# Decode attention over a KV cache: the V transfers are issued from GpSimd's software queue instead of the SP queue

## The chip, the cores and the metric

One core of one Trainium2 chip. The metric is the device time of one execution in microseconds (us).

## The reference

Four layers, alternating between two sets of weights and caches (A, B, A, B). Each has one query token, 32 heads, a head size of 192 and a cache of 8192 positions:

```python
q = layernorm(x) @ wq                  # 640 -> 32 heads x 192
scores = q . k_cache * 192 ** -0.5     # per head, 8192 positions
p = softmax(scores)
o = p @ v_cache
x = x + o @ wo                         # 6144 -> 640
```

Everything is in bfloat16. Nothing of a cache is used twice in a layer, so per head 3.146 MB of K and 3.146 MB of V come from HBM and are used once. Over four layers K and V make 805 MB, the weights 63 MB.

## The kernel before

Every engine has an explicit program of operations and semaphore waits. K and V each have three buffers ("slots") of one head. SP issues all transfers. Cuts are marked with `...`.

```python
def sp_k(h, Kt=Kt):
    i = counters["k"] % NKSLOT                 # NKSLOT = 3
    counters["k"] += 1
    SP.wait(T["kslot"][i])                     # until VectorE is done with head h-3
    ...
    return i, SP.op(f, sem=semK[i], inc=16)    # one transfer of 128 rows of 24,576 bytes

def sp_v(h, Vt=Vt):
    i = counters["v"] % NVSLOT                 # NVSLOT = 3
    counters["v"] += 1
    SP.wait(T["vslot"][i])                     # until TensorE has used V of head h-3
    ...
    return i, SP.op(f, sem=semV[i], inc=16)

# start of a layer (layers 1 to 3)
ev_wq[0], ev_wq[1] = ...                       # two pieces of wq
need_k(0); need_k(1); need_v(0); need_k(2)
ev_wo[0] = sp_wo(0)
# layer normalisation: VectorE, with one power operation on GpSimd
e = PO.op(lambda g: g.tensor_tensor(stat[0:1, 4:5], stat[0:1, 3:4], neghalf[0:1, 0:1], ALU.pow))
...
for h in range(HRUN):
    need_k(h); need_k(h + 1); ...; need_v(h)   # issues what is not issued yet
    cur = stage_tree_a(h, ki, ev_k)            # VectorE: K slot *= q   (waits for K of head h)
    if h >= 1: stage_M(heads[h - 1])
    if h >= 2: stage_out_dve(heads[h - 2])
    stage_tree_a2(cur)                         # VectorE: first halving of the sum
    if h >= 1: stage_softmax(heads[h - 1], ...)  # exponent; TensorE: 64 products with V of head h-1
    stage_act_rows(cur)
    if h >= 2: stage_out(heads[h - 2])         # TensorE: output projection
    stage_tree_b(cur)                          # VectorE: rest of the sum, maximum; frees the K slot
```

So V of head h is needed after VectorE's multiplication for head h+1, about 23 us later than K of head h.

Of the kernel before, what the change touches and what calls it, by code (L numbers as in the profile page):

```python
# [115 lines left out]
def build(nc, A_x, A_k, A_v, A_wq, A_wo, B_x, B_k, B_v, B_wq, B_wo, out, dbg=None, cfg=None):  # L116
# [34 lines left out]
    with ExitStack() as ctx:  # L151
        def sb(name, shape, dt):
            return ctx.enter_context(nc.sbuf_tensor(name, shape, dt))
# [4 lines left out]
        def sem(name):  # L158
            return ctx.enter_context(nc.semaphore(name))

        kslot = [sb(f"kslot{i}", [128, JJ * DH], BF16) for i in range(NKSLOT)]
        vslot = [sb(f"vslot{i}", [128, JJ * DH], BF16) for i in range(NVSLOT)]
# [46 lines left out]
        semV = [sem(f"semV{i}") for i in range(NVSLOT)]  # L209
# [6 lines left out]
        SP = Stream("SP", None)  # L216
# [3 lines left out]
        PO = Stream("POOL", pPOOL)  # L220
# [32 lines left out]
        for i_ in range(2):  # L253
# [5 lines left out]
        T = dict(  # L259
            kslot=[None] * NKSLOT,  # L260
            vslot=[None] * NVSLOT,
            wq=[None] * 2,
            wo=[None] * 2,
            qb=[None, None],
            qslot=[None] * 8,
            sa=[None, None],
            ob=[None, None],
# [16 lines left out]
        for l in range(NL):  # L284
# [30 lines left out]
            def sp_v(h, Vt=Vt):  # L315
                i = counters["v"] % NVSLOT
                counters["v"] += 1
                SP.wait(T["vslot"][i])
                def f(s, i=i, h=h):
                    return s.dma_start(vslot[i][:, :], Vt[0, h].rearrange("(p j) d -> p (j d)", p=128))  # L320
                return i, SP.op(f, sem=semV[i], inc=16)

            ev_wq = [None] * NPAIR
            ev_wo = [None] * NG
# [8 lines left out]
            def need_v(h):  # L333
                if h >= H:
                    return
                if ("v", h) not in kv:
                    kv[("v", h)] = sp_v(h)
# [428 lines left out]
```

## Time and profile before

| what | value | view |
|---|---|---|
| time | 2074.65 us | median of 2 runs |
| DMA engines | busy 9 tenths or more in 39 of 40 slices | slices |
| VectorE / TensorE busy | 85% / 56% | busy table |
| VectorE waiting for K | 213 us in all | waits |
| TensorE waiting for V | 4.4 us in all | waits |
| issue to landing, K / V | 32.6 / 36.1 us | issues |

From the page of the kernel before: the span, busy time by engine (busy us, share, instructions), the DMA share in tenths and GB/s for 40 equal slices, the SP queue (packets, MB, share of 16 engines' span), and the chain of waits by engine.

```profile
span 2073.2 us, 24389 instructions
PE 1158.3 (56%) x9625; PEld 915.1 (44%) x9668; DVE 1764.8 (85%) x1190; ACT 596.1 (29%) x3254; POOL 3.1 (0%) x13
...
DMA  9999999999999999999999999999999999999995
GB/s 395 430 425 428 422 422 427 426 430 419 423 426 425 427 422 424 426 426 428 418 423 426 423 429 424 422 427 426 426 410 425 425 423 424 423 423 425 426 427 254
...
q1 hardware_dynamic: 77700, 868.24, 99.3%
...
DMA 45%; issue 25%; DVE 24%; PE 4%; ACT 1%; SPq 1%; POOL 0%; POOLq 0%; DVEq 0%; ACTq 0%
```

The DMA engines are the bound: they hardly rest, at about 424 GB/s. VectorE, the next busiest, works about 13.8 us per head and waits for K in the rest.

The waits of the kernel before (who waited for whom: us in total, times, longest):

```profile
DVE kslot L463 <- DMA kslot<-in_A_k_cache_dram: 116.6, 56, 8.2
DVE kslot L463 <- DMA kslot<-in_B_k_cache_dram: 96.6, 49, 6.8
...
PE OB L557 <- DMA vslot<-in_B_v_cache_dram: 4.4, 5, 0.9
```

VectorE waits for most heads' K, TensorE waits a little for V.

The chain of waits of the kernel before, its last part (start us, us, what):

```profile
2010.75 32.68 DMA kslot<-in_B_k_cache_dram
2043.45 6.56 DVE kslot L463
```

VectorE starts on the last K (head 31 of layer 3) at 2043.45 us, and the kernel ends 29.7 us later. Between lie that multiplication, the softmax and V product of head 30, then those of head 31.

### The profile page before, as it was taken

The page shows a single profiled execution, that of the slowest core. Times are in us where ns is not written, and L with a number is a line of the kernel's source. Part 1 is how long each engine was busy: PE and PEld are TensorE (multiplying, and loading weights), DVE is VectorE, ACT ScalarE, POOL GpSimd, SP SyncE. Part 2 cuts the span into 40 slices and gives each one's busy share as a digit, 9 for nine tenths or more (in the row PEclk, how much of TensorE's full clock was granted, in tenths as well). Part 3 has the DMA queues.
Part 4 walks back from the last instruction along what each step waited for, and adds up shares of the span by engine and source line. Part 5 has one row for each costly group of instructions (what it writes and reads, how often), then busy time and mean ns, then how long its engine had stood idle before and what let it go on. Part 6 is the DMA issues. An engine that isn't in the chain of part 4 may idle for free.

```text
span 2073.2 us, 24389 instructions
## 1 busy us (share of the span) xinstructions
PE 1158.3 (56%) x9625; PEld 915.1 (44%) x9668; DVE 1764.8 (85%) x1190; ACT 596.1 (29%) x3254; POOL 3.1 (0%) x13
## 2 busy tenths in 40 slices
PE   2565556555465555566536565556563665556656
PEld 1444444444354444444425454445452454444444
DVE  7888888988698888898779888889878988888896
ACT  2222232232232322232223332223222332223232
POOL 0000000000000000000000000000000000000000
PEclk7777777877678777777767777777776777777877
DMA  9999999999999999999999999999999999999995
GB/s 395 430 425 428 422 422 427 426 430 419 423 426 425 427 422 424 426 426 428 418 423 426 423 429 424 422 427 426 426 410 425 425 423 424 423 423 425 426 427 254
DMA packets 77813, 869.79 MB, mean 420 GB/s; under 512 B 4994, under 2 KB 29572, under 8 KB 44932
## 3 DMA queue, kind: packets, MB, share of 16 engines
q1 hardware_dynamic: 77700, 868.24, 99.3%
q8 instruction: 76, 1.25, 0.2%
q14 instruction: 37, 0.30, 0.0%
HBM read 868.22 MB, written 0.00 MB: 419 GB/s over the span
## 4 chain that ended last, share of the span: by engine, by line
DMA 45%; issue 25%; DVE 24%; PE 4%; ACT 1%; SPq 1%; POOL 0%; POOLq 0%; DVEq 0%; ACTq 0%
DMA kslot<-in_B_k_cache_dram 28%; DMA kslot<-in_A_k_cache_dram 17%; DVE kslot L463 12%; DVE kslot L504 5%; DVE kslot L492 4%; PE OB L557 3%; DVE s_sb L508 1%; SPq L312 0%; DVE M_sb L530 0%; DVE m_sb L515 0%; PE QB L412 0%; PE YL L632 0%; ACT p_sb L547 0%; DVE rl_sb L572 0%; SPq L295 0%
## 5 line engine op out<-in xcount | busy, mean ns | idle before, releaser
L463 DVE TENSOR_TENSOR kslot<-kslot,q_sb 128x12288 bf16<-128x12288 bf16 x128 | 839.3, 6557 | 226.2 <-DMA kslot<-in_A_k_cache_dram 116.6
L557 PE MATMUL OB<-vslot,p_sb 128*1 128x192 bf16 x8192 | 951.1, 294 | 84.3 <-ACT p_sb L547 78.6
L557 PEld LDWEIGHTS OB<-vslot,p_sb 128*1 128x1 bf16 x8192 | 809.6, 101 | 205.7 <-ACT p_sb L547 93.5
L539 PE MATMUL SA<-M_bf,ones_bf 1*128 1x1 bf16 x128 | 22.9, 179 | 689.2 <-ACT M_bf L537 689.2
L504 DVE TENSOR_TENSOR kslot<-kslot 128x2688 bf16<-128x2688 bf16 (+2 forms) x384 | 374.4, 975 | 13.3
L492 DVE TENSOR_TENSOR kslot<-kslot 128x5376 bf16<-128x5376 bf16 x128 | 374.7, 2927 | 0.1
L481 ACT ACTIVATE kslot<-kslot 128x192 bf16<-128x192 bf16 x1024 | 355.3, 348 | 22.2 <-DVE kslot L463 22.2
L539 PEld LDWEIGHTS SA<-M_bf,ones_bf 1*128 1x128 bf16 x128 | 12.4, 97 | 725.0 <-ACT M_bf L537 725.0
L537 ACT ACTIVATE M_bf<-M_sb 1x1 bf16<-1x1 f32 x128 | 26.5, 207 | 666.3 <-DVE M_sb L530 666.3
L481 ACT ACTIVATION_READ_ACCUMULATOR kslot<-kslot 128x1 f32 x1024 | 192.1, 188 | 0.0
L508 DVE TENSOR_REDUCE s_sb<-kslot 128x56 f32<-128x672 bf16 x128 | 109.1, 852 | 4.4
L632 PE MATMUL YL<-wo,oT_sb 128*1 128x512 bf16 x256 | 83.0, 378 | 51.8 <-ACT oT_sb L609 31.7
L605 ACT ACTIVATE oT_sb<-OB 128x1 bf16<-128x1 f32 x64 | 11.2, 175 | 310.9 <-PE OB L593 310.9
L608 ACT ACTIVATE oT_sb<-OB 64x1 bf16<-64x1 f32 x64 | 10.9, 170 | 281.0 <-PE OB L597 281.0
L412 PE MATMUL QB<-wq,xT_b 128*128 128x512 bf16 x197 | 57.5, 426 | 11.2 <-issue 6.4
L523 PE MATMUL SA<-ident,m_bf 128*1 128x128 bf16 x128 | 28.2, 221 | 54.5 <-ACT m_bf L520 54.5
L632 PEld LDWEIGHTS YL<-wo,oT_sb 128*1 128x1 bf16 x256 | 20.7, 81 | 79.7 <-ACT oT_sb L609 37.2
L634 PE MATMUL YH<-wo,oT_sb 128*1 128x128 bf16 x256 | 55.9, 218 | 0.0
L425 ACT ACTIVATE q_sb<-QB 128x512 bf16<-128x512 f32 x48 | 28.7, 598 | 93.6 <-PE QB L412 93.6
L578 ACT ACTIVATE orow_bf<-OB,rl_sb 1x192 bf16<-1x192 f32 x128 | 51.0, 399 | 1.7 <-DVE rl_sb L572 1.7
L547 ACT ACTIVATE p_sb<-s_sb,negm_sb 128x64 bf16<-128x64 f32 x128 | 44.8, 350 | 4.1
L530 DVE TENSOR_REDUCE M_sb<-SA 1x1 f32<-1x128 f32 x128 | 34.7, 271 | 12.6 <-PE SA L523 12.6
(50 smaller groups left out, 368.9 us busy)
## 6 DMA issues: line engine op xcount, KB each, us to landing
kslot<-in_A_k_cache_dram SPq DMA_DIRECT2D x64, 3072.0 KB, 32.6
vslot<-in_A_v_cache_dram SPq DMA_DIRECT2D x64, 3072.0 KB, 36.1
kslot<-in_B_k_cache_dram SPq DMA_DIRECT2D x64, 3072.0 KB, 32.6
vslot<-in_B_v_cache_dram SPq DMA_DIRECT2D x64, 3072.0 KB, 36.3
wq<-in_A_wq_dram SPq DMA_DIRECT2D x12, 1280.0 KB, 24.9
wo<-in_A_wo_dram SPq DMA_DIRECT2D x16, 960.0 KB, 38.2
wq<-in_B_wq_dram SPq DMA_DIRECT2D x12, 1280.0 KB, 25.7
wo<-in_B_wo_dram SPq DMA_DIRECT2D x16, 960.0 KB, 38.6
```

The costliest lines, as they stand in the source:

```text
L412: return t.matmul(QB[nb % 2][:, 0:ncols], lhsT=xT_b[:, c, :], rhs=wq_buf[s_][:, c, (nb % 2) * 512:(nb % 2) * 512 + ncols], start=(c == 0), ...
L463: e = DV.op(lambda v, k3=k3, qb_ap=qb_ap: v.tensor_tensor(k3, k3, qb_ap, ALU.mult))
L481: ea = AC.op(lambda a, k3=k3, par=par, j=j: a.activation(k3[:, j, :], k3[:, j, :], ACT.Copy, accum_out=s_sb[par][:, j:j + 1]))
L492: e = DV.op(lambda v, kt=kt, hw_=hw_: v.tensor_tensor(kt[:, :, 0:hw_], kt[:, :, 0:hw_], kt[:, :, hw_:DH], ALU.add))
L504: e = DV.op(lambda v, kt=kt, hw_=hw_, w=w: v.tensor_tensor(kt[:, :, 0:hw_], kt[:, :, 0:hw_], kt[:, :, hw_:w], ALU.add))
L508: cur["s"] = DV.op(lambda v, kt=kt, par=par, w=w, JA=JA: v.tensor_reduce(s_sb[par][:, JA:JJ], kt[:, :, 0:w], AX.X, ALU.add))
L539: cur["negM"] = PE.op(lambda t, par=par: t.matmul(SA[par][:, SA_NEGM:SA_NEGM + 1], lhsT=ones_bf[0:1, 0:128], rhs=M_bf[par][0:1, 0:1], star ...
L547: cur["p"] = AC.op(lambda a, par=par: a.activation(p_sb[par][:], s_sb[par][:], ACT.Exp, bias=negm_sb[par][:], scale=C))
L557: return t.matmul(OB[par][0:1, 0:DH], lhsT=p_sb[par][:, j:j + 1], rhs=vs3[:, j, :], start=(j == 0), stop=(j == JJ - 1))
L578: cur["orow"] = AC.op(lambda a, par=par: a.activation(orow_bf[par][:], OB[par][0:1, 0:DH], ACT.Copy, scale=rl_sb[par][0:1, 0:1]), tag=(f"O ...
L632: return t.matmul(YL[0:1, 0:512], lhsT=lhsT, rhs=rhs[:, 0:512], start=st, stop=sp_)
L634: return t.matmul(YH[0:1, 0:D - 512], lhsT=lhsT, rhs=rhs[:, 512:D], start=st, stop=sp_)
```

## The change

The intent: SP issues everything in one program order, so a V transfer whose slot is not free holds up the K transfer behind it, and the other way round. GpSimd is idle (busy 3.1 us). Giving it the V transfers lets each stream wait for its own slots only.

```diff
             def sp_v(h, Vt=Vt):
                 i = counters["v"] % NVSLOT
                 counters["v"] += 1
-                SP.wait(T["vslot"][i])
+                PO.wait(T["vslot"][i])
                 def f(s, i=i, h=h):
                     return s.dma_start(vslot[i][:, :], Vt[0, h].rearrange("(p j) d -> p (j d)", p=128))
-                return i, SP.op(f, sem=semV[i], inc=16)
+                return i, PO.op(f, sem=semV[i], inc=16)
```

## The prediction

> **What bounds the kernel.** The DMA engines. The slices show DMA at 9 tenths in all but the last, mostly 422 to 430 GB/s; the queue table gives the SP queue 99.3% of 16 engines' span. VectorE is busy 85%, TensorE 56%. The chain of waits is 45% "DMA into kslot", and the waits view has VectorE waiting 213 us for K and TensorE only 4.4 us for V. Per head VectorE works about 13.8 us; K and V (3.146 MB each) take about 14.8 us together at 424 GB/s, near 16 us with the weights. Packet records: a K or V row is one 24,576-byte packet of 915 ns; the 1,280- and 2,048-byte weight packets take 58 and 87 ns.
>
> **What the change does.** No byte and no compute instruction is removed; VectorE, ScalarE and TensorE keep their order. 128 of SP's 306 commands move to GpSimd; SP's saving is not on the path, as the queue behind it is never empty.
>
> What moves is order. Before, K and V are served first in, first out. After, each engine alternates between two queues packet by packet (the Trainium skill, "DMA: Bandwidth & Descriptors", section "Queues, rings and completion order"; no run shows it yet). K and V packets are equal, so they share half and half; V runs ahead until its three slots are full. Against small weight packets V takes nearly the whole engine, so the first weights, and K behind them, come later (by up to some 15 us), DMA still busy. The GpSimd stream also holds the power operation of each layer's normalisation, so V of heads 1 and 2 of a layer waits for it. At the first boundary the timeline gives about 9 MB outstanding at VectorE's last reduction (517 us); 7.2 MB can move before the power operation (534 us): little or no bubble.
>
> **What of it is on the path.** In the body, DMA stays saturated, so the time per head stays. The end changes: before, the last K is used at 2043.5 us and DMA ends near 2052.5 us, V last; then VectorE, softmax and the V product run to 2073. After, the last K and V share the engines, so K can land up to 8 to 9 us later, and everything after it too: my estimate +7 us. Start and boundaries: +0 to +8. Descriptor work on GpSimd is hidden by three slots. VectorE runs almost only two-input tensor operations and reductions here; the skill's "SBUF — State Buffer", section "Who interferes with whom", infers these do not block descriptor writing.
>
> **Predicted time: 2084 us, 8 in 10 within 2066 to 2114.** Faster by over 2%: 0.02; within 2%: 0.85; slower by over 2%: 0.13.
>
> **What would show it.** A second, software queue with about 403 MB; 24,576-byte packets in both; body slices still 420 to 430 GB/s; VectorE's multiplication still 6.56 us; the last K in use near 2050, not 2043.5; no new waits of TensorE for V.
>
> **What would make it wrong.** (1) Software descriptors cut a row into smaller packets: fitting the packet times gives about 12 ns fixed each, so 4 KB packets would cost V about 6%, some 60 us: slower. (2) Descriptor writing is held off by VectorE's nearly continuous work: TensorE would wait for V and DMA would show holes. (3) GpSimd holds up VectorE: its operations would lengthen beyond the 2 us of slack per head. (4) DMA holes at the layer boundaries. (5) Two queues overlap better and lift the rate above 430 GB/s: faster, at most about 1%.

## More of the kernel before

The DMA issues of the kernel before (KB each, median us from issue to landing):

```profile
kslot<-in_A_k_cache_dram SPq DMA_DIRECT2D x64, 3072.0 KB, 32.6
vslot<-in_A_v_cache_dram SPq DMA_DIRECT2D x64, 3072.0 KB, 36.1
```

Stretches of 5 us in the second layer, 20 to 35 us after its first multiplication (busy us and instructions by engine, TensorE clock, DMA share, GB/s):

```profile
core 0: us, PE busy (x) PEld busy (x) DVE busy (x) ACT busy (x) POOL busy (x), PEclk, DMA share, GB/s
560.00:565.00 5.00, 3.88 (x25) 3.02 (x26) 4.93 (x4) 3.50 (x19) 0.00 (x0) 0.50 1.05 417
565.00:570.00 5.00, 3.89 (x44) 3.59 (x42) 4.90 (x5) 0.52 (x3) 0.00 (x0) 0.94 1.01 426
```

The DMA share stays at 1: there is no hole after the pause between two layers.

## The result, and the profile after

2096.3 us (2 runs: 2095.62 and 2096.99), correct. The ratio to the kernel before is 1.0104, with a 95% interval of 1.0075 to 1.0133. Ratios in this document are the mean time of one kernel's fast runs over that of the other's fast runs of the same rounds, so not quite the ratio of the medians that are quoted.

From the page of the kernel after, the lines that answer to those of before:

```profile
span 2093.8 us, 24432 instructions
PE 1153.6 (55%) x9668; PEld 909.6 (43%) x9668; DVE 1760.3 (84%) x1190; ACT 593.7 (28%) x3254; POOL 71.6 (3%) x141
...
DMA  9999999999999999999999999999999999999993
GB/s 400 423 428 427 424 420 428 428 426 421 421 393 427 425 425 422 427 425 430 421 391 428 425 427 423 424 425 425 427 424 390 426 424 423 430 424 425 427 425 162
...
q1 hardware_dynamic: 59268, 465.58, 53.4%
q0 software_dynamic: 18432, 402.66, 45.0%
```

Same bytes, same busy time, same rate in most slices. Four slices are lower: those with 393, 391 and 390 GB/s, one near the start of each of layers 1 to 3, and the last one (162 against 254).

The waits of the kernel after:

```profile
DVE kslot L463 <- DMA kslot<-in_A_k_cache_dram: 134.3, 27, 19.6
DVE kslot L463 <- DMA kslot<-in_B_k_cache_dram: 102.6, 26, 13.0
```

VectorE's wait for K grew from 213 to 237 us, in half as many and longer waits. TensorE's wait for V is no longer in the list.

The issues of the kernel after:

```profile
kslot<-in_A_k_cache_dram SPq DMA_DIRECT2D x64, 3072.0 KB, 30.1
vslot<-in_A_v_cache_dram POOLq DMA_DIRECT2D x64, 3072.0 KB, 19.6
```

V now lands 19.6 us after its issue instead of 36.1, though nobody waited for it before. K hardly gained.

The chain of waits of the kernel after, its last part:

```profile
2029.88 33.74 DMA kslot<-in_B_k_cache_dram
2063.64 6.56 DVE kslot L463
```

The last K is used at 2063.64 us, 20.2 us later than before; the rest of the kernel takes 30.1 us, against 29.7 before. So nearly all of the loss of 20.6 us lies ahead of that point.

Stretches after the first multiplication of the second layer (now at 553.7 us):

```profile
core 0: us, PE busy (x) PEld busy (x) DVE busy (x) ACT busy (x) POOL busy (x), PEclk, DMA share, GB/s
570.00:575.00 5.00, 0.18 (x1) 0.10 (x1) 5.00 (x3) 0.54 (x3) 0.00 (x0) 0.50 1.02 419
575.00:580.00 5.00, 4.77 (x31) 3.84 (x32) 4.90 (x4) 2.94 (x17) 0.00 (x0) 0.52 0.71 305
580.00:585.00 5.00, 2.97 (x38) 2.81 (x35) 4.93 (x4) 0.51 (x3) 0.53 (x1) 1.00 0.65 211
585.00:590.00 5.00, 1.26 (x9) 0.95 (x9) 5.00 (x4) 1.85 (x10) 0.00 (x0) 0.67 0.98 423
```

Here are the holes: a DMA share of 0.71 and 0.65 while VectorE is fully busy.

**Where the 20.6 us of the two profiles are.** The following is worked out from the trace: a transfer has landed when its semaphore gets its sixteenth increment; "early" is the mean time from landing to use, over heads 3 to 31 of each layer (use of K: VectorE's multiplication starts; use of V: the exponent that feeds the product ends).

| | before | after |
|---|---|---|
| K early | 0.4 us | 2.8 us |
| V early | 0.8 us | 20.3 us |
| last K or V transfer lands (DMA ends) | 2058.0 us | 2064.5 us |
| last K used | 2043.5 us | 2063.6 us |
| last K used before DMA ends | 14.5 us | 0.9 us |
| span after DMA ends | 15.2 us | 29.3 us |

DMA ends 6.5 us later, and what is left after it is 14.1 us longer; together 20.6. The first is for the most part the holes: from the packet records, between 20 us and DMA's end, the idle time of the engines came to 8.2 us before (5.0 of it in the last 10 us) and 13.4 after (2.6 in the last 10 us). So the holes outside the last 10 us grew from 3.2 to 10.8 us, the engines' idle time in the last 10 us shrank, and 1.3 of the 6.5 us are not accounted for by idle time. The second is the order at the end: before, the last V landed last; after, the last K landed 0.9 us before DMA ends.

**How the queues share an engine.** The packet records show it best at the start of the kernel after. The number of packets that ended in each stretch:

| stretch | V queue, 24,576-byte packets | SP queue, packets |
|---|---|---|
| 12 to 16 us | 35 | 36 of K, 24,576 bytes |
| 26 to 28 us | 32 | 32 of wq, 2,048 bytes |
| 30 to 32 us | 32 | 32 of wq, 2,048 bytes |

As many packets of one queue are served as of the other, whatever their sizes. Beside K, V gets half of the bytes. Beside wq, V gets 92% (24,576 of 26,624 bytes), and the K transfers that stand behind wq in the SP queue wait as long. V of head 0 had landed at 21.4 us and was first used at 57.6. The second piece of wq landed at 39.8 us instead of 18.2, and the first multiplication started at 26.2 us instead of 14.8.

### The profile page after: what moved, and what is told of

Read it like the earlier page. It is cut to its first block, busy times and chain, and to the rows that moved or that the text cites. A ratio compares the mean times of both kernels' runs of the same rounds, so it can differ in the third digit from the quotient of the medians.

```text
span 2093.8 us, 24432 instructions
## 1 busy us (share of the span) xinstructions
PE 1153.6 (55%) x9668; PEld 909.6 (43%) x9668; DVE 1760.3 (84%) x1190; ACT 593.7 (28%) x3254; POOL 71.6 (3%) x141
## 4 chain that ended last, share of the span: by engine, by line
DVE 46%; DMA 46%; PE 6%; ACT 1%; issue 1%; SPq 0%; POOL 0%; DVEq 0%; ACTq 0%
DMA kslot<-in_A_k_cache_dram 25%; DVE kslot L463 24%; DMA kslot<-in_B_k_cache_dram 21%; DVE kslot L504 9%; DVE kslot L492 9%; PE OB L557 5%; DVE s_sb L508 3%; DVE M_sb L530 1%; DVE m_sb L515 1%; PE QB L412 1%; PE YL L632 0%; ACT p_sb L547 0%; DVE rl_sb L572 0%; ACT M_bf L537 0%; SPq L295 0%
## 5 line engine op out<-in xcount | busy, mean ns | idle before, releaser
L557 PE MATMUL OB<-vslot,p_sb 128*1 128x192 bf16 x8192 | 938.9, 292 | 82.1 <-ACT p_sb L547 82.1
L537 ACT ACTIVATE M_bf<-M_sb 1x1 bf16<-1x1 f32 x128 | 26.2, 204 | 689.7 <-DVE M_sb L530 689.7
L608 ACT ACTIVATE oT_sb<-OB 64x1 bf16<-64x1 f32 x64 | 10.8, 168 | 273.2 <-PE OB L597 273.2
L412 PE MATMUL QB<-wq,xT_b 128*128 128x512 bf16 x240 | 67.8, 423 | 7.4 <-DMA wq<-in_A_wq_dram 4.7
L320 POOL DMA_DIRECT2D vslot<-in_A_v_cache_dram x64 | 34.3, 537 | 944.0 <-PE OB L593 443.9
L320 POOL DMA_DIRECT2D vslot<-in_B_v_cache_dram x64 | 34.2, 535 | 936.6 <-PE OB L593 457.6
## 6 DMA issues: line engine op xcount, KB each, us to landing
kslot<-in_A_k_cache_dram SPq DMA_DIRECT2D x64, 3072.0 KB, 30.1
vslot<-in_A_v_cache_dram POOLq DMA_DIRECT2D x64, 3072.0 KB, 19.6
```

The lines of the kernel that those rows point to most:

```text
L320: return s.dma_start(vslot[i][:, :], Vt[0, h].rearrange("(p j) d -> p (j d)", p=128))
L412: return t.matmul(QB[nb % 2][:, 0:ncols], lhsT=xT_b[:, c, :], rhs=wq_buf[s_][:, c, (nb % 2) * 512:(nb % 2) * 512 + ncols], start=(c == 0), ...
L557: return t.matmul(OB[par][0:1, 0:DH], lhsT=p_sb[par][:, j:j + 1], rhs=vs3[:, j, :], start=(j == 0), stop=(j == JJ - 1))
```

## The experiments

The theories, as they stood ahead of the first run:

- **A, the order of service.** A second queue lets V run ahead of K. V fills its slots with data that nobody needs yet; K comes last at the end, and after a layer's pause DMA runs out of free slots. Who fills the queue is immaterial.
- **B, the software queue itself**: descriptor work on GpSimd, its port to SBUF, its packets.
- **C, GpSimd's program**: V of heads 1 and 2 of a layer waits behind the power operation, and that makes the holes.
- **D** (came up later), **a second queue as such**: alternation costs, whatever each queue holds.

All runs gave correct results and were timed for 5 rounds. The kernel before ran in the same rounds. "Early", "DMA ends" and "last K" are worked out as above, from the one profiled execution of each run.

| run | median us | ratio to before (95%) | K early | V early | DMA ends | last K used before DMA ends |
|---|---|---|---|---|---|---|
| before | 2075.22 to 2075.66 | | 0.4 | 0.8 | 2058.0 | 14.5 |
| c0_after_again | 2094.92 | 1.0094 (1.0080 to 1.0108) | 2.7 | 20.9 | 2066.9 | 0.1 |
| e1_v_act | 2097.66 | 1.0108 (1.0093 to 1.0124) | 3.5 | 19.5 | 2063.6 | -1.0 |
| e2_all_gpsimd | 2076.75 | 1.0007 (0.9995 to 1.0020) | 0.4 | 0.8 | 2059.5 | 14.5 |
| e3_v_before_pow | 2093.31 | 1.0087 (1.0072 to 1.0103) | 2.8 | 20.5 | 2064.9 | 2.5 |
| e4_gate_ends | 2084.62 | 1.0047 (1.0034 to 1.0059) | 3.1 | 19.4 | 2059.1 | 7.5 |
| e5_gate_last | 2089.61 | 1.0070 (1.0057 to 1.0084) | 2.9 | 20.4 | 2065.7 | 7.6 |
| e6_gate_inner | 2089.95 | 1.0073 (1.0059 to 1.0086) | 2.8 | 19.6 | 2059.1 | 0.9 |
| e9_gate_k_same | 2081.90 | 1.0032 (1.0020 to 1.0045) | 1.9 | 5.3 | 2059.2 | 8.5 |
| e8_gate_k_next | 2078.65 | 1.0014 (1.0001 to 1.0026) | 7.8 | -1.8 | 2058.1 | 10.6 |
| e7_gate_start | 2098.76 | 1.0111 (1.0096 to 1.0126) | 3.0 | 20.4 | 2069.3 | 1.7 |
| e10_k_alone_sp | 2092.33 | 1.0084 (1.0069 to 1.0099) | 12.2 | -0.8 | 2074.0 | 9.3 |
| e11_k_alone_gpsimd | 2094.48 | 1.0091 (1.0075 to 1.0108) | 12.2 | -1.1 | 2072.3 | 9.7 |

### The change again, with more rounds

No edit.

> The changed kernel unaltered, as a control with more rounds: 1.0104 times the kernel before (about 2096 us), as the first two runs gave. All theories agree.

2094.92 us over four runs (2090.75 to 2098.15). The loss is well clear of noise; single runs of this kernel differ by up to 7.4 us, where those of the kernel before stay within 1.3 in the same rounds.

### V from ScalarE's hardware queue

```diff
-                PO.wait(T["vslot"][i])
+                AC.wait(T["vslot"][i])
 ...
-                return i, PO.op(f, sem=semV[i], inc=16)
+                return i, AC.op(f, sem=semV[i], inc=16)
 ...
             T["sa"][0] = ev_xTb
+            need_v(1); need_v(2)
 ...
                     stage_out_dve(heads[h - 2])
+                    need_v(h + 1)        # right after ScalarE has waited for that V product anyway
```

The two added calls keep the moment of issue close to that of the change: within 5.1 us for all V but the first of layers 1 to 3, which came some 26 us later here.

> V from ScalarE's hardware queue, issued at the same moments as GpSimd issues it in the changed kernel (after the V product that frees the slot). Theory A (the order of service: a second queue lets V run ahead of K, whoever fills it): the loss stays, 2090 to 2102 us, DMA holes of about 3 us after each layer start, the last K in use 20 us later than before. Rival B (the software queue itself: descriptor work on GpSimd, its port, its packets): back to 2072 to 2080 us.

2097.66 us. The queue table and an issue line of this run:

```profile
q1 hardware_dynamic: 59268, 465.58, 53.4%
q10 hardware_dynamic: 18432, 402.66, 45.0%
...
vslot<-in_A_v_cache_dram ACTq DMA_DIRECT2D x64, 3072.0 KB, 19.5
```

No software queue is left, and the loss is whole: V again lands 19.5 us after issue, and the last K is used after DMA has ended. Rival B can't explain this run.

### Everything from GpSimd's software queue

```diff
 def sp_wq, sp_wo:
-                QE = AC if cfg.get("...", False) else SP
+                QE = PO
 def sp_k:
-                SP.wait(T["kslot"][i])
+                PO.wait(T["kslot"][i])
 ...
-                return i, SP.op(f, sem=semK[i], inc=16)
+                return i, PO.op(f, sem=semK[i], inc=16)
```

> K, V and both weights all from GpSimd, so one queue again, first in first out, in the order of the kernel before, but all through the software queue. Theory A: back to 2072 to 2082 us. Rival B: twice the bytes through the software queue, so the loss at least stays, 2096 to 2120 us.

2076.75 us; the interval of the ratio includes 1. The queue table and the issues:

```profile
q0 software_dynamic: 51584, 868.24, 99.0%
...
kslot<-in_A_k_cache_dram POOLq DMA_DIRECT2D x64, 3072.0 KB, 32.4
vslot<-in_A_v_cache_dram POOLq DMA_DIRECT2D x64, 3072.0 KB, 38.3
```

All 868 MB through the software queue cost at most 0.2%. With one queue, first in first out, K and V are as early as before (0.4 and 0.8 us), and the last K is used 14.5 us before DMA ends, as before. This run and the one above it turn each other's two properties round: the kind of queue is immaterial, the number of queues is not. B has fallen.

### V ahead of the power operation

```diff
-                need_k(1); need_v(0); need_k(2)
+                need_k(1); need_v(0); need_k(2); need_v(1); need_v(2)      # layer 0; so also in the others
```

> The changed kernel with V of heads 1 and 2 of each layer ahead of the power operation in GpSimd's stream, so that nothing holds them but their slots. Theory A (order of service): nothing gained, 2091 to 2099 us, holes after each layer start as before. Rival C (the power operation holds them and makes the holes): the holes go, 2084 to 2090 us.

2093.31 us. In the second layer V of heads 1 and 2 was now issued at 532.72 and 542.66 us; in the change both followed the power operation at 548.84. The same stretches of this run:

```profile
575.00:580.00 5.00, 4.36 (x29) 3.39 (x29) 4.90 (x4) 3.28 (x18) 0.00 (x0) 0.50 0.68 290
580.00:585.00 5.00, 3.33 (x41) 3.15 (x38) 4.93 (x4) 0.51 (x3) 0.57 (x1) 0.99 0.55 167
```

The hole is no smaller than in the change. A likely reason, not tested, is that what is issued earlier also lands earlier, and so leaves nothing more to do when DMA runs dry. C has fallen.

### A gate at the end of each layer, and its two parts

The gate holds V of heads 29 to 31 until K that is needed sooner has landed. It only adds waits.

```diff
                 PO.wait(T["vslot"][i])
+                if h >= H - 3:                                   # e4_gate_ends
+                if h >= H - 3 and l == NL - 1:                   # e5_gate_last, instead
+                if h >= H - 3 and l < NL - 1:                    # e6_gate_inner, instead
+                    PO.wait(kv[("k", min(h + 1, H - 1))][1])
```

All layers:

> The changed kernel, still V on the software queue, but in each layer V of head 29 also waits until K of head 30 has landed, and V of heads 30 and 31 until K of head 31 has. Theory A: K of head 31 lands sooner in each layer, the DMA holes after the layer starts and the longer end both go: 2068 to 2080 us. Rival B: no gain, 2094 to 2104 us. Rival C (V of heads 1 and 2 held behind the power operation makes the holes): the end is mended, the holes stay: 2082 to 2088 us.

2084.62 us: half of the loss is gone, but not all, as theory A had it (2068 to 2080); a miss in size. The trace shows why. At the end of the last layer VectorE was now the one behind: it ran without a pause from 2010.4 us on, while the last K landed at 2040.0 and was used only at 2051.6. V had run ahead through the other 29 heads of each layer as before (19.4 us early on the mean), so VectorE, it seems, came to the gate late; no run tested this reason.

The last layer alone:

> The gate of the gated kernel (V of heads 29 to 31 waits for K of head 30 or 31) in the last layer alone. Theory A: only the end is mended. From the gated kernel's trace, where the last K is used 7.5 us before DMA ends against 0.9 us in the changed kernel, the gain is about 6.6 us: 2086 to 2091 us, with the three holes still there.

2089.61 us, inside the range. DMA ends at 2065.7 us, so its holes are untouched, but the last K is used 7.6 us before that instead of 0.1.

The first three layers alone:

> The same gate in the first three layers alone. Theory A: only the holes shrink. In the gated kernel DMA ended 5.4 us sooner than in the changed one, so the gain is about 5 us: 2088 to 2092 us, the last K still landing last of all.

2089.95 us, inside the range. Here it is the other way round: DMA ends at 2059.1 us, 7.8 us sooner than in the repeated change, and the last K is still used only 0.9 us before. The stretches in which the change had its first hole, in e5_gate_last:

```profile
575.00:580.00 5.00, 4.62 (x33) 3.75 (x34) 4.90 (x4) 3.10 (x17) 0.00 (x0) 0.55 0.70 300
580.00:585.00 5.00, 2.87 (x36) 2.71 (x33) 4.93 (x4) 0.51 (x3) 0.53 (x1) 1.00 0.63 202
```

And the same stretches in e6_gate_inner, without the hole (smaller ones came later in the layers: 1.2 us were lost between 780 and 790 us, and 2.3 between 1810 and 1820):

```profile
575.00:580.00 5.00, 0.85 (x12) 0.69 (x9) 5.00 (x1) 0.31 (x2) 0.53 (x1) 0.93 0.96 413
580.00:585.00 5.00, 3.15 (x20) 2.45 (x21) 4.97 (x5) 3.75 (x20) 0.00 (x0) 0.50 1.04 447
```

The two parts gain 5.3 and 5.0 us against the repeated change (2094.92), together 10.3; both gates in one kernel gain 10.3. The profiles show that these are two separate costs of the same order of service: one gate moves the last K and not DMA's end, the other DMA's end and not the last K. That they add up so exactly is chance: the intervals of the ratios of the repeated change, e5_gate_last and e6_gate_inner overlap a little, so each gain of 5 us is uncertain by some 4 us.

### A gate on every head

```diff
                 PO.wait(T["vslot"][i])
+                if h > 0:
+                    PO.wait(kv[("k", h)][1])                     # e9_gate_k_same
+                    PO.wait(kv[("k", min(h + 1, H - 1))][1])     # e8_gate_k_next, instead
```

Until K of the same head has landed:

> The changed kernel with V of every head but a layer's first held until K of the same head has landed. Theory A: V's lead over its use (20 us in the changed kernel, 0.8 us before) falls to 5 to 12 us, and the time falls most of the way, 2074 to 2086 us. Rival B: 2093 to 2100 us.

2081.90 us: V's lead fell from 20 to 5.3 us, and two thirds of the loss went.

Until K of the next head has landed:

> The changed kernel with V of every head but a layer's first held until K of the next head has landed, one step harder than the gate on the same head (2081.9 us, V 5.3 us early). Theory A: V comes just in time, K first as in one queue, so the loss goes: 2071 to 2079 us, unless V now comes late; then TensorE would wait for V by some us per head and the time would rise above the softer gate's.

2078.65 us, against 2075.22 for the kernel before on the same chip. V is now used 1.8 us before it has landed, on the mean, which is to say that TensorE waits for it (the added lines move line 557 to 559; us in total, times, longest):

```profile
PE OB L559 <- DMA vslot<-in_A_v_cache_dram: 210.3, 31, 13.1
PE OB L559 <- DMA vslot<-in_B_v_cache_dram: 174.5, 25, 11.9
```

385 us of waiting on TensorE cost next to nothing, as TensorE is not the bound. The fear that such waits would lift the time above that of the softer gate was wrong. With V on a second queue, and that a software queue, nearly all of the loss is gone once V is held back (the interval of the ratio, 1.0001 to 1.0026, leaves 0.2 to 5.4 us).

### A gate at the start only

```diff
                 PO.wait(T["vslot"][i])
+                if h <= 2 and l == 0:
+                    PO.wait(kv[("k", min(h + 1, H - 1))][1])
```

> The changed kernel with the hard gate on the first three V of the first layer alone (V of heads 0, 1, 2 waits for K of heads 1, 2, 3). V of head 0 now stands before the power operation, which therefore waits too. Theory A: DMA is busy either way, so where in the first layer the first multiplication starts costs nothing: unchanged, 2091 to 2099 us. Had the later first multiplication (26 against 15 us) been part of the loss, or were the start sensitive, it would move by 5 us or more.

2098.76 us, within the range that was written, but the experiment does not show what it was meant to. The power operation stands behind the gated V, so the first multiplication came later still, at 34.4 us instead of 26.2, and two new holes of 2.4 and 2.1 us opened near 60 and 140 us. In the change itself no 10 us stretch from 20 us to the first layer's end lost more than half a microsecond. So a later start need not be free, and at 26 us it opened no hole of its own; whether it adds to the later ones is left open.

### K alone on a queue, twice

If the trouble is that K stands behind the weights while V does not, then K should have the queue of its own. First the weights join V on GpSimd:

```diff
 def sp_wq, sp_wo (from the kernel after):
-                QE = AC if cfg.get("...", False) else SP
+                QE = PO
```

> Two queues still, but the weights go with V to GpSimd and K has the SP queue alone. Theory A in full (the loss comes from V having a queue without the weights, so that it gets ahead of K, which stands behind them): K is now the one that runs ahead, V comes later, and the loss goes: 2068 to 2080 us, no holes after the layer starts, the last K used 15 us or more before DMA ends. If a second queue as such costs (rival D: alternation between queues), it stays at 2088 to 2100 us.

Then the mirror of the change: only K moves to GpSimd, V and the weights stay on SP.

```diff
 def sp_k (from the kernel before):
-                SP.wait(T["kslot"][i])
+                PO.wait(T["kslot"][i])
 ...
-                return i, SP.op(f, sem=semK[i], inc=16)
+                return i, PO.op(f, sem=semK[i], inc=16)
```

> The mirror of the change: K instead of V moves to GpSimd's software queue; V and the weights stay on SP. Theory A: which kind of queue carries K does not matter, so as the run with K alone on SP, 2068 to 2080 us, and the two within 0.3% of each other. Rival B: it carries the same bytes through the software queue as the change, so the same loss, 2090 us or more.

2092.33 and 2094.48 us: a clear miss of theory A as it was put. TensorE's waits for V in the first of the two:

```profile
PE OB L557 <- DMA vslot<-in_A_v_cache_dram: 201.7, 33, 11.7
PE OB L557 <- DMA vslot<-in_B_v_cache_dram: 161.4, 24, 12.0
```

Its issues of K and V of A:

```profile
kslot<-in_A_k_cache_dram SPq DMA_DIRECT2D x64, 3072.0 KB, 19.2
vslot<-in_A_v_cache_dram POOLq DMA_DIRECT2D x64, 3072.0 KB, 37.8
```

And its stretches after the first multiplication of the second layer, which came at 556.5 us:

```profile
575.00:580.00 5.00, 2.24 (x15) 1.75 (x16) 4.97 (x4) 2.84 (x16) 0.00 (x0) 0.50 1.00 418
580.00:585.00 5.00, 5.00 (x45) 4.39 (x43) 4.86 (x6) 0.85 (x5) 0.00 (x0) 0.70 0.26 84
585.00:590.00 5.00, 0.91 (x12) 0.75 (x10) 5.00 (x1) 0.30 (x2) 0.55 (x1) 0.98 0.91 359
```

K and V have changed places: K lands 19.2 us after issue and is 12.2 us early, V comes late. The loss is the same, by another split. The end is no longer K's (the last K is used 9.3 us before DMA ends), but DMA itself ends at 2074.0 us, 9.5 later than after the change. The holes are larger: 20.6 us idle against 13.4. The two runs are about 0.1% apart, so again the kind of queue is immaterial.

So it is not that K has to go first. The stream without the weights runs ahead, whichever it is, and both are hurt by that. Theory D would also fit these two runs, but not e8_gate_k_next and e9_gate_k_same, which have two queues and lose 0.14% and 0.32%; nor e4_gate_ends, where the queues alternate freely in 29 of 32 heads of each layer and DMA ends only some 1.2 us later than before. One quantity to compare is how many slots hold data that has landed and is not yet used up. Worked out from landings and uses (a K slot held until 13.7 us after its multiplication starts, a V slot until 7.2 us after its product starts: lengths read from the traces), the mean from 20 us to DMA's end, of six slots (good to some 0.02):

| run | K slots | V slots | both | idle DMA, us |
|---|---|---|---|---|
| before | 0.94 | 0.55 | 1.49 | 8.2 |
| e2_all_gpsimd | 0.93 | 0.55 | 1.48 | 9.0 |
| e9_gate_k_same | 1.02 | 0.88 | 1.90 | 7.2 |
| e8_gate_k_next | 1.36 | 0.57 | 1.93 | 5.7 |
| e11_k_alone_gpsimd | 1.74 | 0.68 | 2.42 | 20.5 |
| e10_k_alone_sp | 1.76 | 0.69 | 2.45 | 20.6 |
| after | 1.11 | 1.78 | 2.89 | 13.4 |
| e1_v_act | 1.19 | 1.70 | 2.89 | 11.4 |

A slot that holds data early is not available to DMA. Between two layers VectorE can't use any K: from the last multiplication of a layer to the first of the next, 36 to 37 us pass before and after the change (48 to 49 with K alone, where V holds up the end of the layer). Where slots are mostly empty, DMA spends that pause filling them. Where they are full, it fills the rest and then waits for VectorE or TensorE to free the next one.

The mean over the execution does not settle this by itself. By the same working e4_gate_ends and e6_gate_inner, left out of the table, hold 2.83 and 2.81 slots, nearly as many as the change, and yet from a layer's last multiplication to 45 us after the next layer's first, DMA lost no time in either (9.9 us over the three boundaries in the change, 1.6 before). What their gates lowered is the content as the pause begins: over the 13.7 us from a layer's last multiplication 2.3 slots are full on the mean, against 2.9 in the change and 1.5 before. The two runs with K alone hold only 2.0 to 2.1 there, but their pause is 12 us longer. So it is the content at the pause, together with the length of the pause, that fits all of these runs. This account was formed after they ran, and no further run tested it, nor more slots, nor the weights on a queue of their own.

## Why the prediction was right or wrong

The time was inside the range: 2084 us was forecast, within 2066 to 2114, and 2096.3 came, slower by 1.0% and within 2%. The size was not well forecast: the middle of the range was a loss of 9.4 us, and 21.6 came, over twice that. It is the width of the range, and not the sum, that covered this. Point by point:

- **The body stays saturated at the same rate: right.** Most slices have 420 to 430 GB/s in both kernels; packets of 24,576 bytes take 915 ns on the hardware queue and 916 on the software queue.
- **Nothing from the software queue itself: right, and shown.** e2_all_gpsimd carries everything through it at +0.07%. VectorE's multiplication had a median of 6.558 us before and 6.549 after. The Trainium skill, "SBUF — State Buffer", section "Who interferes with whom", infers that two-input tensor operations do not hold off descriptor writing; this trace agrees.
- **Packet-by-packet alternation: right, and shown**, 32 packets against 32 with sizes of 24,576 and 2,048 bytes. This is what the Trainium skill says in "DMA: Bandwidth & Descriptors", section "Queues, rings and completion order" ("at *packet* granularity"). The forecast that the first weights and K come later held too: the first multiplication moved by 11.4 us.
- **The longer end: the right mechanism, half the size.** This is the term that was mis-sized: "K can land up to 8 to 9 us later, and everything after it too: my estimate +7 us". The part after DMA's end grew by 14.1 us. The bound of 8 to 9 us came from reading DMA's end as 2052.5 us off a coarse stretch; by its landings the last V came at 2058.0, so the last K had 14.5 us to lose, and it lost 13.6 of them. (From 2055 to 2060 us only 10 GB/s were still moved: most engines were done by then, but a transfer has landed only with the last of its sixteen increments.) That K and V would finish side by side held: the last K landed at 2063.6 us, the last V at 2064.5. e5_gate_last shows this term by itself: 5.3 us of it come back with three waits in the last layer.
- **"Start and boundaries: +0 to +8": inside the range, but "little or no bubble" was wrong.** DMA ended 6.5 us later. The count of outstanding bytes was made up to the power operation, and there DMA was indeed busy. The hole came 20 to 30 us after the first multiplication, when the three V slots were full and K had only the slot that VectorE had just freed. The count took the slots' state from the trace of before, where V is 0.8 us early, not 20. e6_gate_inner shows this term by itself (5.0 us), and e3_v_before_pow that the power operation has no part in it.
- **The last K in use near 2050 us: wrong**, it was 2063.6, by the two terms above.

## What to carry to other kernels

In a kernel like this one, where transfers are the bound, the program order of one queue is a schedule: it brought each buffer just in time and kept slots empty for the next pause. Splitting that queue gives the order away to an alternation by packets, in which the stream that has no short-packet transfers ahead of it ran ahead, and a slot that holds data early is lost for as long. Before splitting, look at how long before its use each stream lands: here nobody waited for V, and a queue of its own for it only took from K; a wait on the landing of the K that is needed sooner won nearly all of the loss back.

## What the Trainium skill lacked or had wrong

- "DMA: Bandwidth & Descriptors", sections "Issuing engines are not separate DMA queues" and "Rules for kernel authors": that spreading transfers over issuing engines only saves issue time. Here it changes the order of service, which cost 1.0% (2074.65 to 2096.3 us) at an unchanged rate in most slices, and by the same amount from ScalarE's hardware queue (1.08%). The page doesn't say that it can cost.
- The same page, "Queues, rings and completion order": alternation is by packets, with typical packets of several descriptors. Here one row is one packet, of 2,048 or of 24,576 bytes; 32 of one alternated with 32 of the other, so the queue with short rows got 8% of the bytes. The page draws no consequence for queues with rows of unequal length.
- The same page, "SWDGE vs HWDGE vs iDMA", has packets of 4,096 bytes or less as preferred on the software queue. Here it moved 24,576-byte rows as single packets (916 ns), and in e2_all_gpsimd it put short rows together: two of 2,048 bytes in one packet of 4,096 (173 ns, against 87 each on the hardware queue), four of 1,280 in one of 5,120 (229 ns, against 58 each).
- "SBUF — State Buffer", the summary of rules, says to estimate HBM transfers with 358 GB/s, and does not say for how many running cores. This program, on one core, moved 420 to 430 GB/s in most slices of 2 ms; for such a case the figure is too low.
